# Four attention layers on one core: the range test and its branch moved to the end, loads reordered, masks and normalisations moved from POOL to DVE

## Chip, cores and metric

One core of a Trainium2 chip (trn2). The metric is the device time of one execution in microseconds (us), median of several runs; the profile is of one execution. TensorE is called PE, its weight loads PEld, VectorE DVE, ScalarE ACT, GpSimd POOL, and SyncE, which issues most DMAs, SP; a q behind an engine's name (SPq) marks its sequencer, here mostly for the issue of a DMA. "Slot" is a step of the kernel's own software pipeline in an A layer: a group of four heads takes six slots, and a segment of 512 tokens has eight groups G.

## The reference, cut to what matters

```python
x = A_x                                              # 2048 tokens x 640, bf16
x = x + _A_ref(_layernorm(x), wq, wk, wv, wo, beta)  # 4 segments of 512, 32 heads of 20, causal,
x = x + _B_ref(_layernorm(x), mem0, Wq, Wk, Wv, Wo)  #   plus a linear memory gated by sigmoid(beta)
x = x + _A_ref(_layernorm(x), ...)                   # B: 64 steps of 32 tokens, 32 heads of 128,
x = x + _B_ref(_layernorm(x), ...)                   #   8 memory tokens carried from step to step
```

The B layers are a chain of 64 steps each; the A layers have a short chain of four segments. A segment needs the LayerNorm of its 512 tokens, transposed, before its first projection.

## The kernel before

It first computes from wq and wk a bound on the scores. If the bound holds, exponentials need no row maximum, and each A layer branches to a short arm:

```python
# in prep_A: pad wq and wk to 32 columns per head, sums of squares on POOL and DVE, ... (cut)
flag = tp_.tile([1, 1], mybir.dt.int32, name="a_flag")
nc.vector.tensor_copy(flag[:], b2[:])
W.bounded = nc.values_load(flag[0:1, 0:1])
...
# at the end of layer_A
with tc.If(W.bounded > 0) as arm:
    run(False, None)
with arm.Else():
    ...
```

In an A layer the next segment's LayerNorm is threaded through the groups of this one. `tt` counts its four tiles of 128 tokens. Statistics are made on DVE, the power -0.5 on POOL, the normalisation on POOL, the transposes on PE:

```python
def ln_stats(nc, xt):
    ...                                    # two bn_stats, bn_aggr, add eps, all on DVE
    nc.gpsimd.tensor_tensor(out=rstd[:], in0=rstd[:], in1=C.mhalf[:, 0:1], op=ALU.pow)
    return mv, rstd
...
for tt in range(4):
    if (G, slot) == (tt + 1, 1):
        ln[tt] = ln_load(n + 1, tt)
    if (G, slot) == (tt + 2, 2):
        mv, rstd = ln_stats(nc, ln[tt])
        ln[tt] = ln_apply(nc.gpsimd, ln[tt], mv, rstd)
    if (G, slot) == (tt + 3, 4):
        ln_tr(nc, ln.pop(tt), n + 1, tt)
```

Inside the layers the kernel pins each compute engine's order of instructions to the order of these lines; DMA issues are left to the compiler's scheduler. The causal mask is applied to the exponentials by POOL, in four selects for each pair of heads (one, one and two for the three parts of the scores):

```python
nc.scalar.activation(out=PT[:], in_=Sx[:, :, 0:N], func=ACT.Exp, scale=SC)
for c0 in ((0,), (0,), (0, 256))[part]:
    v = PT[:, :, c0:c0 + 128]
    nc.gpsimd.affine_select(out=v, in_=v, ...)
```

A B layer begins with its 5 MB output weight and only then asks for its first tokens:

```python
nc.sync.dma_start(WB.wo[:], B_Wo.rearrange("h e d -> e h d"))   # in the caller
layer_B(...)                # its start: ln_dma(0); ln_norm(0); ln_tr(0)
```

## Time and profile before

Before the prediction the kernel took 3148.21 us (median of 3 runs, 3141.85 to 3148.53). I cut the span at four kinds of event, each of them twice: the first projection a_PP of an A layer, the end of its last output matmul a_YP, the first b_Qa of a B layer and the end of its last b_OPSd.

| stretch | us before |
|---|---|
| start, to the first a_PP | 61.7 |
| first A layer | 303.2 |
| A to B, first time | 58.8 |
| first B layer | 1158.7 |
| B to A | 33.1 |
| second A layer | 306.6 |
| A to B, second time | 60.9 |
| second B layer | 1159.1 |
| end | 5.6 |

The names in the profiles: a_xt is a tile of x, a_xn its normalised form, a_tps the transposes of that on PE; a_PP are the projections, a_S the scores, a_PT the exponentials, a_VP and a_vaug the values, a_pv their product with a_PT, a_YP the output matmul and a_xo its sum with x, a_UP the update of the memory. In B, b_xt and b_lntps are what a_xt and a_tps are in A.

The start, from the timeline of the kernel before. The columns are start, duration, engine, line, operation, output and inputs, shape and count; in brackets the idle time before it and what ended it.

```profile
8.11 15.77 DVE L135 COPY a_pad_100<-a_raw_98 128x640 bf16<-128x640 bf16 x3 [1.96 <-DMA a_raw_98<-in_A_wq_dram]
...
32.58 0.14 DVE L151 CAST a_flag<-a_b_144 1x1 int32<-1x1 f32 x1
...
43.16 2.51 POOL L228 TENSOR_SCALAR a_xn<-a_xt,a_mv,a_rstd 128x640 bf16<-128x640 bf16 x1 [0.25 <-POOL a_rstd L223]
...
61.66 2.10 PE L84 MATMUL a_PP<-a_xnT_193,a_wt 128*128 128x512 bf16 x9 [0.24 <-PE a_VP L241]
```

Padding and the bound take 33 us before anything of the attention begins, and LayerNorm, half of it on POOL, follows.

The two A layers before, in the view of windows (stretch, its length, busy time of each engine, granted PE clock, share of DMA, GB/s):

```profile
core 0: us, PE busy (x) PEld busy (x) DVE busy (x) ACT busy (x) POOL busy (x), PEclk, DMA share, GB/s
61.70:364.90 303.20, 265.34 (x2789) 139.30 (x2818) 170.85 (x416) 200.19 (x272) 179.56 (x358) 0.91 0.41 133
1615.50:1922.20 306.70, 265.40 (x2789) 138.89 (x2818) 171.57 (x416) 200.40 (x272) 180.54 (x359) 0.92 0.32 98
```

What PE and the weight loads waited for in the first A layer before, besides "issue" (view of waits: engine and what it waited for, us in total, times, longest):

```profile
PEld L84 <- POOL a_PT L84: 28.7, 76, 1.5
PE a_pv L84 <- POOL a_PT L84: 13.8, 35, 1.2
```

These are POOL's selects.

The change from A to B before, timeline:

```profile
373.46 0.39 SPq L1041 DMA_DIRECT2D b_wo<-in_B_Wo_dram  x1
374.03 9.31 SPq L617 DMA_DIRECT2D b_xt<-xres_bf  x1
...
391.49 0.89 DVE L84 BATCH_NORM_STATS2 b_ln_st<-b_xt 128x6 f32<-128x320 bf16 x2 [16.90 <-DMA b_xt<-xres_bf]
...
394.10 0.69 PE L84 MATMUL b_lntps<-c_identb,b_xt 128*128 128x128 bf16 x5 [29.25 <-DMA b_XOd<-xres]
```

The tile b_xt is asked for just after Wo and lands 17 us later; PE stands for 29 us.

### The profile page before, as it was taken

To read this page: it belongs to the slowest core of one execution; us is meant where nothing else is said; L and a number is where in the kernel's file an instruction comes from. 1 tells how busy PE (TensorE), PEld (TensorE's weight loads), DVE (VectorE), ACT (ScalarE), POOL (GpSimd) and SP (SyncE) were. 2 spreads that over 40 slices of the span, in tenths; PEclk is the share of its full clock that TensorE was granted. 3 is DMA by queue.
4 is the path that set the end of the run, shared out by engine and by line. 5 is a ranking of instruction groups with operands and counts; after the bars stand their busy time and mean duration, and the time that the engine had idled before them with its cause. 6 is when DMAs were issued, how large, how long until landed. Compare 5 with 4: busy or idle time off the path is not lost. (4 is left out here: it accounts for less than half of the span.)

```text
span 3147.7 us, 118684 instructions
## 1 busy us (share of the span) xinstructions
PE 2734.2 (87%) x52376; PEld 1461.4 (46%) x52438; DVE 1626.5 (52%) x4137; ACT 1328.7 (42%) x2798; POOL 756.3 (24%) x1975
## 2 busy tenths in 40 slices
PE   3889479999999999999868884899999999999997
PEld 1444235545555454455434442445455455455554
DVE  5665335555555555555446652455555555555554
ACT  2766324443433443433337662343433433434432
POOL 4666311111111111111136652111111111111111
PEclk9998789999999999999979995999999999999998
DMA  4633400000000000000023333000000000000000
GB/s 165 213 97 98 131 14 17 19 18 18 18 17 18 19 17 18 17 18 16 13 85 118 114 97 108 12 16 16 16 15 16 16 15 16 15 16 17 13 14 10
DMA packets 110982, 134.33 MB, mean 43 GB/s; under 512 B 30704, under 2 KB 96240, under 8 KB 108528
## 3 DMA queue, kind: packets, MB, share of 16 engines
q1 hardware_dynamic: 110304, 126.55, 13.9%
q8 instruction: 414, 6.78, 0.9%
q14 instruction: 120, 0.98, 0.1%
q10 hardware_dynamic: 144, 0.01, 0.0%
HBM read 91.84 MB, written 26.25 MB: 38 GB/s over the span
## 5 line engine op out<-in xcount | busy, mean ns | idle before, releaser
L84 PEld LDWEIGHTS <-b_hT 128*32 128x32 bf16 x15520 | 355.5, 96 | 375.7 <-DVE b_hT L84 46.5
L84 POOL TENSOR_TENSOR b_P<-b_Pu,b_rs 128x256 bf16<-128x256 bf16 (+1 forms) x256 | 111.6, 457 | 1180.0 <-DVE b_rs L84 1172.7
L84 ACT ACTIVATE a_PT<-a_S 128x768 bf16<-128x768 f32 (+1 forms) x384 | 328.8, 888 | 103.8 <-PE a_S L84 91.4
L84 PE MATMUL b_OPS<-b_wo,b_OTsb 128*32 128x320 bf16 x8192 | 317.5, 310 | 44.7 <-DVE b_OTsb L84 44.7
L84 PE MATMUL b_V<-b_wv,b_hT 128*32 128x512 bf16 x5120 | 346.8, 382 | 0.0
L84 PEld LDWEIGHTS <-b_OTsb 128*32 128x32 bf16 x8192 | 212.8, 99 | 118.5 <-DVE b_OTsb L84 58.3
L84 ACT ACTIVATE b_Pu<-b_SP 128x320 bf16<-128x320 f32 x256 | 112.0, 437 | 357.0 <-DVE b_SP L84 357.0
L84 POOL TENSOR_SCALAR_AFFINE_SELECT a_PT<-a_PT 128x256 bf16<-128x256 bf16 x512 | 207.2, 425 | 175.6 <-ACT a_PT L84 173.3
L84 ACT COPY b_QT<-b_TPQ 128x128 bf16<-128x128 bf16 x508 | 178.2, 379 | 119.7 <-PE b_TPQ L84 115.9
L84 DVE COPY b_KT<-b_TPK 128x128 bf16<-128x128 bf16 x382 | 101.8, 267 | 217.9 <-PE b_TPK L84 217.9
L84 PE MATMUL b_Qa<-b_wq,b_hT 128*32 128x512 bf16 x2560 | 163.5, 384 | 34.7 <-DVE b_hT L84 34.7
L84 DVE CAST b_hT<-b_MT 128x24 bf16<-128x24 f32 x126 | 23.1, 183 | 329.6 <-PE b_MT L84 329.6
L84 ACT CAST b_msb<-b_OPS 128x320 bf16<-128x320 f32 x128 | 54.5, 426 | 296.1 <-PE b_OPS L84 296.1
L84 POOL COPY b_OTdef<-b_OTsb 128x256 bf16<-128x256 bf16 x128 | 51.0, 399 | 509.0 <-DVE b_OTsb L84 509.0
L84 DVE CAST b_Ksb<-b_Ka 128x512 bf16<-128x512 f32 x128 | 88.6, 692 | 149.0 <-PE b_Ka L84 148.8
L84 PE MATMUL b_Ka<-b_wk,b_hT 128*32 128x512 bf16 x2560 | 161.8, 382 | 0.0
L84 PE MATMUL b_Kb<-b_wk,b_hT 128*32 128x512 bf16 x2560 | 161.6, 381 | 0.0
L84 DVE TENSOR_REDUCE b_negmax<-b_SP 128x8 f32<-128x320 f32 x256 | 124.8, 487 | 71.1 <-PE b_SP L84 71.1
L84 DVE TENSOR_REDUCE b_ssum<-b_Pu 128x8 f32<-128x320 bf16 x256 | 123.2, 481 | 72.4 <-ACT b_Pu L84 72.4
L84 PE MATMUL b_Qb<-b_wq,b_hT 128*32 128x512 bf16 x2560 | 160.3, 379 | 0.0
L84 ACT ACTIVATE b_Qsb<-b_Qb 128x512 bf16<-128x512 f32 x128 | 76.4, 597 | 197.2 <-PE b_Qb L84 197.2
L84 DVE CAST b_Ksb<-b_Kb 128x512 bf16<-128x512 f32 x128 | 88.6, 692 | 125.8 <-PE b_Kb L84 125.8
(224 smaller groups left out, 5105.0 us busy)
## 6 DMA issues: line engine op xcount, KB each, us to landing
b_wo<-in_B_Wo_dram SPq DMA_DIRECT2D x2, 5120.0 KB
b_Vt<-b_Vtb SPq DMA_DIRECT2D x512, 16.0 KB
b_XO<-xres SPq DMA_DIRECT2D x256, 30.0 KB
a_wvo<-in_A_wo_dram SPq DMA_DIRECT2D x8, 800.0 KB
b_wq<-in_B_Wq_dram SPq DMA_DIRECT2D x5, 1024.0 KB
b_wk<-in_B_Wk_dram SPq DMA_DIRECT2D x5, 1024.0 KB
b_wv<-in_B_Wv_dram SPq DMA_DIRECT2D x5, 1024.0 KB
xres<-a_xo SPq DMA_DIRECT2D x16, 320.0 KB
```

The source lines that it names most:

```text
L84: r = f(*a, **k)
```

## The change

The intent: no test and no branch ahead of the work. The sums of exponentials and their inverses are totalled as the A layers run, and tested at the very end; if one is out of range, all four layers are done again with row maxima. Around this the loads are reordered (x first; in B the tokens ahead of Wo), the pads are used from SBUF in the first layer, and DVE takes work from POOL: two of the four selects become one minimum with a 0-or-huge mask, and the normalisations. The normalisation is also placed one group later, and its load five slots later. The core of the diff, cut:

```diff
+def watch(nc, C, sums, inverses):
+    n = sums.shape[1]
+    nc.gpsimd.tensor_tensor(out=C.tot[:, 0, 0:n], in0=C.tot[:, 0, 0:n], in1=sums, op=ALU.add)
+    nc.gpsimd.tensor_tensor(out=C.tot[:, 1, 0:n], in0=C.tot[:, 1, 0:n], in1=inverses, op=ALU.add)
 ... (cut: pads filled after the first LayerNorms, out_of_range() with a matmul over C.tot and a value load)
-                for c0 in ((0,), (0,), (0, 256))[part]:
+                if part == 2 and not general:
+                    v = PT[:].rearrange("p j (b q) -> p j b q", q=128)[:, :, 0:3:2, :]
+                    nc.vector.tensor_tensor(out=v, in0=v, in1=tri[:]..., op=ALU.min)
+                for c0 in ((0,), (0,), (0, 256) if general else ())[part]:
 ... (cut)
-                        if (G, slot) == (tt + 1, 1):
+                        if (G, slot) == (tt + 2, 0):
                             ln[tt] = ln_load(n + 1, tt)
-                        if (G, slot) == (tt + 2, 2):
+                        if (G, slot) == (tt + 3, 2):
                             mv, rstd = ln_stats(nc, ln[tt])
-                            ln[tt] = ln_apply(nc.gpsimd, ln[tt], mv, rstd)
+                            ln[tt] = ln_apply(nc.vector, ln[tt], mv, rstd)
                         if (G, slot) == (tt + 3, 4):
                             ln_tr(nc, ln.pop(tt), n + 1, tt)
 ... (cut: layer_B)
-        ln_dma(0); ln_norm(0); ln_tr(0)
+        ln_dma(0)
+        m0 = wk.tile([8, D], BF16, name="b_m0", tag="OTsb")
+        nc.sync.dma_start(m0[:], mem0)
+        for q in range(4):
+            nc_raw.sync.dma_start(W.wo[:, 8 * q:8 * q + 8, :], wo_src[:, 8 * q:8 * q + 8, :])
+        ln_norm(0); ln_tr(0)
 ... (cut: full_kernel)
+        run(False)
+        with tc.If(out_of_range(nc, tc, C) > 0):
+            run(True)
```

More of the change, by code (lines that the diff above doesn't have):

```diff
@@ L52, in build_consts @@
     nc.vector.memset(C.mhalf[:], -0.5)
+    C.tot = cp.tile([128, 2, 16], F32, name="c_tot")
+    nc.vector.memset(C.tot[:], 0.0)
     tctx.close()
@@ L102, in __getattr__, with out_of_range @@
         return getattr(self._nc, attr)
+def watch(nc, C, sums, inverses):
+    n = sums.shape[1]
+    nc.gpsimd.tensor_tensor(out=C.tot[:, 0, 0:n], in0=C.tot[:, 0, 0:n], in1=sums, op=ALU.add)
+    nc.gpsimd.tensor_tensor(out=C.tot[:, 1, 0:n], in0=C.tot[:, 1, 0:n], in1=inverses, op=ALU.add)
+def out_of_range(nc, tc, C):
+    with ExitStack() as tctx:
+        tp_ = tctx.enter_context(tc.tile_pool(name="c_range", bufs=1))
+        pp = tctx.enter_context(tc.tile_pool(name="c_range_ps", bufs=1, space=PSUM))
+        ok = tp_.tile([128, 32], F32, name="c_ok")
+        nc.vector.tensor_scalar(out=ok[:], in0=C.tot[:].rearrange("p k n -> p (k n)"), scalar1=1e30, scalar2=None, op0=ALU.is_le)
+        ones = tp_.tile([128, 1], F32, name="c_one")
+        nc.vector.memset(ones[:], 1.0)
+        ps = pp.tile([1, 32], F32, name="c_okps")
+        nc.tensor.matmul(ps[:], lhsT=ones[:], rhs=ok[:], start=True, stop=True)
+        n = tp_.tile([1, 1], F32, name="c_n")
+        nc.vector.tensor_reduce(out=n[:], in_=ps[:], axis=AX.X, op=ALU.add)
+        nc.vector.tensor_scalar(out=n[:], in0=n[:], scalar1=-1.0, scalar2=128.0 * 32, op0=ALU.mult, op1=ALU.add)
+        flag = tp_.tile([1, 1], mybir.dt.int32, name="c_flag")
+        nc.vector.tensor_copy(flag[:], n[:])
+        return nc.values_load(flag[0:1, 0:1])
@@ L105, with prep_A, fill @@
 class AWeights:
     pass
-def prep_A(nc, tc, C, A_wq, A_wk, A_beta):
-    SC = 1.0 / math.sqrt(20.0)
-    W = AWeights()
-    W.gates = tc.dram_tile([128, 64], F32, name="a_gates")
-    W.wpad = [tc.dram_tile([2, 128, NCH * 128], BF16, name=f"a_wpad{G}") for G in range(8)]
-    with ExitStack() as tctx:
-        tp_ = tctx.enter_context(tc.tile_pool(name="a_prep", bufs=1))
-        pp = tctx.enter_context(tc.tile_pool(name="a_prep_ps", bufs=1, space=PSUM))
-        bb = tp_.tile([128, 32], BF16, name="a_beta_bf")
-        with nc.allow_non_contiguous_dma(reason="beta bcast"):
-            nc.scalar.dma_start(bb[:], A_beta.partition_broadcast(128))
-        hs = tp_.tile([128, 2, 32], F32, name="a_hs")
-        for k, src in enumerate((A_wq, A_wk)):
-            raw = tp_.tile([128, NCH, D], BF16, name=f"a_raw{k}")
-            nc.sync.dma_start(raw[:], src.rearrange("(c p) n -> p c n", p=128))
-            pad = tp_.tile([128, 8, NCH, 4, 32], BF16, name=f"a_pad{k}")
-            nc.gpsimd.memset(pad[:], 0.0)
+def prep_A(nc, tc, W, space, A_wq, A_wk, A_beta):
+    raw = space[:, 0:2 * NCH * D].rearrange("p (k c n) -> p k c n", k=2, c=NCH)
+    n0 = 2 * NCH * D
+    pad = space[:, n0:n0 + 2 * NCH * 1024].rearrange("p (k g c h s) -> p k g c h s", k=2, g=8, c=NCH, h=4)
+    for k in range(2):
+        nc.gpsimd.memset(pad[:, k, :, :, :, 20:32].rearrange("p g c h s -> p (g c h) s"), 0.0)
+    for k, src in enumerate((A_wq, A_wk)):
+        nc.scalar.dma_start(raw[:, k], src.rearrange("(c p) n -> p c n", p=128))
+    W.pad = [[pad[:, k, G].rearrange("p c h s -> p c (h s)") for k in range(2)] for G in range(8)]
+    def fill():
+        for k in range(2):
@@ L129, in prep_A @@
             for c in range(NCH):
-                dst = pad[:, :, c, :, 0:20]
-                s_ = raw[:, c, :].rearrange("p (g h d) -> p g h d", g=8, d=20)
-                if c % 2:
+                dst = pad[:, k, :, c, :, 0:20]
+                s_ = raw[:, k, c, :].rearrange("p (g h d) -> p g h d", g=8, d=20)
+                if c % 3 == 1:
                     nc.scalar.copy(dst, s_)
@@ L135, in prep_A @@
                     nc.vector.tensor_copy(dst, s_)
-            for G in range(8):
-                nc.sync.dma_start(W.wpad[G][k], pad[:, G].rearrange("p c h d -> p (c h d)"))
-            sq = tp_.tile([128, NCH, D], F32, name=f"a_sq{k}")
-            nc.gpsimd.tensor_tensor(out=sq[:], in0=raw[:], in1=raw[:], op=ALU.mult)
-            nc.vector.tensor_reduce(out=hs[:, k, :], in_=sq[:].rearrange("p c (h d) -> p h c d", d=20), axis=AX.XY, op=ALU.add)
-        ones = tp_.tile([128, 1], F32, name="a_ones")
@@ L142, in prep_A @@
-        nc.vector.memset(ones[:], 1.0)
-        hp = pp.tile([1, 2, 32], F32, name="a_hp")
-        nc.tensor.matmul(hp[:], lhsT=ones[:], rhs=hs[:].rearrange("p k h -> p (k h)"), start=True, stop=True)
-        mx = tp_.tile([1, 2], F32, name="a_mx")
-        nc.vector.tensor_reduce(out=mx[:], in_=hp[:], axis=AX.X, op=ALU.max)
-        b2 = tp_.tile([1, 1], F32, name="a_b2")
-        nc.vector.tensor_tensor(out=b2[:], in0=mx[:, 0:1], in1=mx[:, 1:2], op=ALU.mult)
-        nc.vector.tensor_scalar(out=b2[:], in0=b2[:], scalar1=(40.0 / (1.02 * 640.0 * SC)) ** 2, scalar2=None, op0=ALU.is_le)
@@ L150, in prep_A @@
-        flag = tp_.tile([1, 1], mybir.dt.int32, name="a_flag")
-        nc.vector.tensor_copy(flag[:], b2[:])
-        W.bounded = nc.values_load(flag[0:1, 0:1])
-        e = tp_.tile([128, 32], F32, name="a_beta_e")
-        nc.scalar.activation(out=e[:], in_=bb[:], func=ACT.Exp, scale=-1.0)
-        nc.vector.tensor_scalar(out=e[:], in0=e[:], scalar1=1.0, scalar2=None, op0=ALU.add)
-        gg = tp_.tile([128, 2, 32], F32, name="a_gg0")
-        nc.vector.reciprocal(out=gg[:, 1, :], in_=e[:])
+        for G in range(8):
+            for k in range(2):
+                nc.sync.dma_start(W.wpad[G][k], pad[:, k, G].rearrange("p c h s -> p (c h s)"))
@@ new lines, in gates @@
+    def gates(pool):
+        bb = pool.tile([128, 32], BF16, name="a_beta_bf")
+        with nc.allow_non_contiguous_dma(reason="beta bcast"):
+            nc.scalar.dma_start(bb[:], A_beta.partition_broadcast(128))
+        gg = pool.tile([128, 2, 32], F32, name="a_gg")
+        nc.scalar.activation(out=gg[:, 0, :], in_=bb[:], func=ACT.Exp, scale=-1.0)
+        nc.vector.tensor_scalar(out=gg[:, 0, :], in0=gg[:, 0, :], scalar1=1.0, scalar2=None, op0=ALU.add)
+        nc.vector.reciprocal(out=gg[:, 1, :], in_=gg[:, 0, :])
@@ L158, in prep_A, with layer_A @@
         nc.vector.tensor_scalar(out=gg[:, 0, :], in0=gg[:, 1, :], scalar1=-1.0, scalar2=1.0, op0=ALU.mult, op1=ALU.add)
-        nc.sync.dma_start(W.gates[:], gg[:].rearrange("p k h -> p (k h)"))
-    return W
-def layer_A(nc_raw, tc, C, W, A_wv, A_wo, x_src, x_dst, xb_dst, src_is_bf16, prefetch=()):
+        return gg
+    W.gates = gates
+    return fill
+def layer_A(nc_raw, tc, C, W, A_wv, A_wo, x_src, x_dst, xb_dst, src_is_bf16, general, prep=None, prefetch=()):
     SC = 1.0 / math.sqrt(20.0)
@@ L182, in layer_A @@
         phik = [st.tile([128, 4, 4, 32], BF16, name=f"a_phik{i}") for i in range(2)]
-        for i in range(2):
-            nc_raw.gpsimd.memset(vaug[i][:, :, :, 20:22], 1.0)
-            nc_raw.gpsimd.memset(phik[i][:], 0.0)
         xnTs = [st.tile([128, NCH, 512], BF16, name=f"a_xnT{i}") for i in range(2)]
@@ L192, in load_vo, with wload @@
             nc_raw.sync.dma_start(wvo[:], src.rearrange("(c p) n -> p c n", p=128))
-        load_vo(A_wv)
-        bd = st.tile([128, 4, 21], BF16, name="a_bd")
-        nc_raw.vector.memset(bd[:], 0.0)
-        for j in range(4):
-            nc_raw.vector.memset(bd[32 * j:32 * j + 32, j, :], 1.0)
-        eps = st.tile([128, 2, 4, 4], F32, name="a_eps")
-        nc_raw.vector.memset(eps[:, 0], 0.0)
-        nc_raw.vector.memset(eps[:, 1], 1e-6)
-        gg = st.tile([128, 2, 32], F32, name="a_gg")
-        nc_raw.sync.dma_start(gg[:].rearrange("p k h -> p (k h)"), W.gates[:])
         class Seg:
             pass
+        def wload(u):
+            if prep and u < NG:
+                wts[u] = W.pad[u]
+                return
+            wt = wk.tile([128, 2, NCH, 128], BF16, name="a_wt")
+            for k in range(2):
+                nc_raw.sync.dma_start(wt[:, k].rearrange("p c m -> p (c m)"), W.wpad[u % NG][k])
+            wts[u] = [wt[:, 0], wt[:, 1]]
         def ln_load(n, tt):
@@ L243, in vproj @@
             nc.vector.tensor_copy(vaug[n % 2][:, tt, 16 * half:16 * half + 16, 0:20], VP[:].rearrange("p (h d) -> p h d", d=20))
-        for tt in range(4):
-            xt = ln_load(0, tt)
-            mv, rstd = ln_stats(nc_raw, xt)
-            ln_tr(nc_raw, ln_apply((nc_raw.vector, nc_raw.gpsimd)[tt % 2], xt, mv, rstd), 0, tt)
+        xts = [ln_load(0, tt) for tt in range(2)]
+        fill_pads = prep() if prep else None
+        load_vo(A_wv)
+        wts = {}
+        if not prep:
+            wload(0); wload(1)
+        for i in range(2):
+            nc_raw.gpsimd.memset(vaug[i][:, :, :, 20:22], 1.0)
+            nc_raw.gpsimd.memset(phik[i][:], 0.0)
+        tri = st.tile([128, 128], BF16, name="a_tri")
+        nc_raw.vector.memset(tri[:], 3.0e38)
+        nc_raw.gpsimd.affine_select(out=tri[:], in_=tri[:], pattern=[[1, 128]], compare_op=ALU.is_ge,
+                                    fill=0.0, base=0, channel_multiplier=-1)
+        for tt in range(4):
+            if tt + 2 < 4:
+                xts.append(ln_load(0, tt + 2))
+            mv, rstd = ln_stats(nc_raw, xts[tt])
+            ln_tr(nc_raw, ln_apply(nc_raw.vector, xts[tt], mv, rstd), 0, tt)
+        if fill_pads:
+            fill_pads()
         for tt in range(4):
@@ L251, in layer_A, with run @@
                 vproj(nc_raw, 0, tt, half)
-        def run(general, gctx):
+        bd = st.tile([128, 4, 21], BF16, name="a_bd")
+        nc_raw.vector.memset(bd[:], 0.0)
+        for j in range(4):
+            nc_raw.vector.memset(bd[32 * j:32 * j + 32, j, :], 1.0)
+        eps = st.tile([128, 2, 4, 4], F32, name="a_eps")
+        nc_raw.vector.memset(eps[:, 0], 0.0)
+        nc_raw.vector.memset(eps[:, 1], 1e-6)
+        gg = W.gates(st)
+        def run(gctx):
             nc = _OrdNC(tc, nc_raw, engines=ORDER_ENGINES)
@@ L266, in run @@
                 nc.vector.memset(ones[:], 1.0)
-            wts, us, xin = {}, {}, {}
-            def wload(u):
-                wt = wk.tile([128, 2, NCH, 128], BF16, name="a_wt")
-                for k in range(2):
-                    nc_raw.sync.dma_start(wt[:, k].rearrange("p c m -> p (c m)"), W.wpad[u % NG][k])
-                wts[u] = wt
+            us, xin = {}, {}
             def proj(u, k):
@@ L283, in proj @@
                 for c in range(NCH):
-                    nc.tensor.matmul(PP[:], lhsT=wts[u][:, k, c, :], rhs=xnTs[n % 2][:, c, :], start=(c == 0), stop=(c == NCH - 1))
+                    nc.tensor.matmul(PP[:], lhsT=wts[u][k][:, c, :], rhs=xnTs[n % 2][:, c, :], start=(c == 0), stop=(c == NCH - 1))
                 nc.vector.tensor_copy(U.qk[:, k, :], PP[:])
@@ L354, in score @@
                 nc.scalar.activation(out=PT[:], in_=Sx[:, :, 0:N], func=ACT.Exp, scale=SC)
-                for c0 in ((0,), (0,), (0, 256))[part]:
+                if part == 2 and not general:
+                    v = PT[:].rearrange("p j (b q) -> p j b q", q=128)[:, :, 0:3:2, :]
+                    nc.vector.tensor_tensor(out=v, in0=v, in1=tri[:].unsqueeze(1).unsqueeze(1).to_broadcast([128, 2, 2, 128]), op=ALU.min)
+                for c0 in ((0,), (0,), (0, 256) if general else ())[part]:
                     v = PT[:, :, c0:c0 + 128]
@@ L393, in norm @@
                 nc.vector.tensor_tensor(out=r[:, 0:K], in0=pv[:, 0:K, :, :, 20], in1=eps[:, 0:K], op=ALU.add)
-                nc.vector.reciprocal(out=r[:, 0:K], in_=r[:, 0:K])
-                nc.vector.tensor_tensor(out=r[:, 0:K], in0=r[:, 0:K], in1=gg[:, 0:K, 4 * G:4 * G + 4].unsqueeze(2).to_broadcast([128, K, 4, 4]), op=ALU.mult)
+                i = wk.tile([128, 2, 4, 4], F32, name="a_i")
+                nc.vector.reciprocal(out=i[:, 0:K], in_=r[:, 0:K])
+                if not general:
+                    watch(nc, C, r[:, 0].rearrange("p t j -> p (t j)"), i[:, 0].rearrange("p t j -> p (t j)"))
+                q = wk.tile([128, 2, 4, 4], F32, name="a_q")
+                nc.vector.tensor_tensor(out=q[:, 0:K], in0=i[:, 0:K], in1=gg[:, 0:K, 4 * G:4 * G + 4].unsqueeze(2).to_broadcast([128, K, 4, 4]), op=ALU.mult)
                 Ov = Onat[:, :, 80 * G:80 * G + 80].rearrange("p t (j d) -> p t j d", d=20)
                 if n == 0:
-                    nc.vector.tensor_tensor(out=Ov, in0=pv[:, 0, :, :, 0:20], in1=r[:, 0].unsqueeze(3).to_broadcast([128, 4, 4, 20]), op=ALU.mult)
+                    nc.vector.tensor_tensor(out=Ov, in0=pv[:, 0, :, :, 0:20], in1=q[:, 0].unsqueeze(3).to_broadcast([128, 4, 4, 20]), op=ALU.mult)
                 else:
@@ L401, in norm @@
                     nc.vector.tensor_tensor(out=ts[:].rearrange("p k t d -> p (k t) d"), in0=pv[:].rearrange("p k t j s -> p (k t j) s")[:, :, 0:20],
-                                            in1=r[:].rearrange("p k t j -> p (k t j)").unsqueeze(2).to_broadcast([128, 32, 20]), op=ALU.mult)
+                                            in1=q[:].rearrange("p k t j -> p (k t j)").unsqueeze(2).to_broadcast([128, 32, 20]), op=ALU.mult)
                     tv = ts[:].rearrange("p k (t j) d -> p k t j d", j=4)
@@ L489, in extras @@
                     load_vo(A_wo)
-            wload(0); wload(1)
+            if prep:
+                wload(0); wload(1)
             proj(0, 0); proj(0, 1); phi_q(0); phi_k(0)
@@ L524, in run @@
                     extras(u, slot)
-        with tc.If(W.bounded > 0) as arm:
-            run(False, None)
-        with arm.Else():
-            with ExitStack() as gctx:
-                run(True, gctx)
+        with ExitStack() as gctx:
+            run(gctx)
 class BWeights:
@@ L555, in b_slot_of_head, with layer_B @@
     return j, j + 4 * (2 * b + r // 2), r % 2
-def layer_B(nc, tc, C, W, x_src, xb_src, x_dst, mem0, nsteps=64, out_bf16=False):
+def layer_B(nc, tc, C, W, wo_src, x_src, xb_src, x_dst, mem0, nsteps=64, out_bf16=False):
     SCB = 1.0 / math.sqrt(128.0)
@@ L571, in layer_B @@
         wk = st
+        wop = ctx.enter_context(tc.tile_pool(name="b_wo", bufs=1))
+        W.wo = wop.tile([128, 32, D], BF16, name="b_wo")
         pp = ctx.enter_context(tc.tile_pool(name="b_ps", bufs=8, space=PSUM))
@@ L780, in layer_B @@
         assert sorted(HORDER) == list(range(32))
-        ln_dma(0); ln_norm(0); ln_tr(0)
+        ln_dma(0)
[4 more added lines that the diff above has]
+        ln_norm(0); ln_tr(0)
         alloc_h(0)
-        with nc.allow_non_contiguous_dma(reason="mem0 transpose load (tiny)"):
-            for c in range(NCH):
-                nc.sync.dma_start(hT[0][:, c, 24:32], mem0[:, 128 * c:128 * c + 128].rearrange("t p -> p t"))
+        mt = ps_tile([128, NCH, 8], BF16, "b_m0T")
+        for c in range(NCH):
+            nc.tensor.transpose(mt[:, c, :], m0[0:8, 128 * c:128 * c + 128], C.identb[0:8, 0:8])
+        nc.vector.tensor_copy(hT[0][:, :, 24:32], mt[:])
         alloc_qk(0)
@@ L1025, in full_kernel @@
         mem0 = B_mem0.rearrange("b t d -> (b t) d")
+        wo_src = B_Wo.rearrange("h e d -> e h d")
         X = tc.dram_tile([S_TOK, D], F32, name="xres")
@@ L1028, in full_kernel, with prep, run @@
         WB, loads = load_B_weights(nc, tc, ctx, B_Wq, B_Wk, B_Wv)
-        WA = prep_A(nc, tc, C, A_wq, A_wk, A_beta)
-        nl = len(layers)
-        assert layers[0] == "A" and layers[-1] == "B"
-        for li, L in enumerate(layers):
-            lastl = (li == nl - 1)
-            if L == "A":
-                layer_A(nc, tc, C, WA, A_wv, A_wo, xin if li == 0 else X, X, Xb, li == 0, prefetch=loads)
-                loads = []
-            else:
-                with ExitStack() as bctx:
-                    wop = bctx.enter_context(tc.tile_pool(name="b_wo", bufs=1))
-                    WB.wo = wop.tile([128, 32, D], BF16, name="b_wo")
-                    nc.sync.dma_start(WB.wo[:], B_Wo.rearrange("h e d -> e h d"))
-                    layer_B(nc, tc, C, WB, X, Xb, xout if lastl else X, mem0, out_bf16=lastl)
+        WA = AWeights()
+        WA.wpad = [tc.dram_tile([2, 128, NCH * 128], BF16, name=f"a_wpad{G}") for G in range(8)]
+        def prep():
+            return prep_A(nc, tc, WA, WB.wv[:].rearrange("p c n -> p (c n)"), A_wq, A_wk, A_beta)
+        def run(general):
+            nl = len(layers)
+            assert layers[0] == "A" and layers[-1] == "B"
+            for li, L in enumerate(layers):
+                lastl = (li == nl - 1)
+                if L == "A":
+                    first = li == 0 and not general
+                    layer_A(nc, tc, C, WA, A_wv, A_wo, xin if li == 0 else X, X, Xb, li == 0, general,
+                            prep=prep if first else None, prefetch=loads if first else ())
+                else:
+                    layer_B(nc, tc, C, WB, wo_src, X, Xb, xout if lastl else X, mem0, out_bf16=lastl)
+        run(False)
+        with tc.If(out_of_range(nc, tc, C) > 0):
+            run(True)
 @with_exitstack
```

## The prediction

> **What bounds the kernel now.** The program is four layers, A B A B (table by stretch, timeline). PE is busy 87% of the span and 92% or more inside B, whose 18.1 us steps the change does not touch. So it can pay only at the start, at the three layer changes, and inside A (about 290 us each; PE 81 to 90%, POOL 55 to 68%, DVE 55 to 63%).
>
> **Removed or moved, costed from the timeline:**
>
> 1. *Start.* PE's first projection begins at 61.7 us: 33 us of bound test, pad copies and branch value, then loads, then LayerNorm, half of it on POOL (2.5 us each; DVE 0.45). Three DVE pad copies took 15.8 us beside POOL work. [...] Afterwards x is loaded first, without a test. But the order of instructions shows two 1 MB b_wq loads ahead of the third and fourth x tiles, and the wq/wk loads behind the beta exponential. First projection at 27 to 35 us: **-30 us**.
>
> 2. *A to B, twice.* B's first LayerNorm waits 17 us for a 160 KB tile queued behind the 5 MB Wo load; PE is idle from 364.9 to 394.1 and from 1922.3 to 1949.5 us. Afterwards the tile comes first, and the branch region's barrier and jump are gone. The order still puts the last bf16 cast on POOL, which waits for a store (3.5 us), before B's first power, so about 7 us of gap stay: **-46 us** for both, with a little clock. TensorE is granted 0.5 in these gaps, and 20 matmuls take 2.32 us instead of 1.26 after them[...]. The remaining gap still throttles.
>
> 3. *B to A.* 1582.4 to 1615.5 us. Two x tiles are requested earlier, LayerNorm is all on DVE; the other two still queue behind Wv, which waits for the last stores: **-8 us**.
>
> 4. *Inside A.* Per group POOL loses four of eight selects (0.42 us each) and the 2.5 us normalisations, and gets two small totals (about 0.3 us each, estimated from the 0.36 us memory update). DVE gets two minima (0.45 to 0.8 us each, estimated from the 0.43 us phi minimum) and normalisations of 0.45 to 0.6: roughly 75% busy. PE and weight loads waited for POOL selects 30 to 40 us per A layer (view of waits), but ACT and the full PE stand behind: **-15 us** over both layers, uncertain from -45 to +15.
>
> 5. *End.* The test waits for the last stores, then DVE, PE, DVE, a value load and a branch over the second copy. From the old test (31.6 to 33.8 us) and the 2.3 us jump after an A layer: **+5 us**.
>
> Sum: -94 us. **Predicted 3052 us, 8 in 10 between 3015 and 3085.** Chances: faster by over 2% 0.90, within 2% 0.09, slower 0.01.
>
> **What would show it.** First a_PP matmul near 31 us; b_lntps 6 to 9 us after the last a_YP; first a_PP of the second A about 25 us after the last b_OPSd; POOL about 45% in A, DVE about 75%; B steps still 18.1 us; 4 to 7 us after the last output store.
>
> **What would make it wrong.** DVE becoming A's bottleneck through in-order waits for ACT[...]; late b_wv loads waiting for the pads and holding other loads on their queue; a larger A gain if the clock's dips to 0.83 there come from POOL stalls; a costlier final branch.

The marked cuts take out reasons that no trace or run of this case shows. They take no term out of the sum: -30 - 46 - 8 - 15 + 5 = -94 us.

## The result, and the profile after

The kernel after took 3102.76 us (median of 4 runs, 3099.93 to 3103.3), the kernel before in the same comparison 3145.03 us (3140.91 to 3148.53). The ratio is 0.9864, with a 95% interval of 0.9847 to 0.9881: within 2%, and a gain of 42 us in place of the 94 predicted. Here and below a ratio is the mean time of one kernel's runs over the mean of the other's in the same rounds, so not quite the ratio of the medians quoted. Executions over 1.5% slower than the fastest of the same kernel are left out of the means.

| stretch | before | after | difference | predicted |
|---|---|---|---|---|
| start | 61.7 | 31.7 | -30.0 | -30 |
| first A | 303.2 | 313.4 | +10.2 | -15 for both A |
| A to B | 58.8 | 38.1 | -20.7 | -46 for both |
| first B | 1158.7 | 1158.0 | -0.7 | 0 |
| B to A | 33.1 | 28.4 | -4.7 | -8 |
| second A | 306.6 | 317.4 | +10.8 | (above) |
| A to B | 60.9 | 40.4 | -20.5 | (above) |
| second B | 1159.1 | 1160.0 | +0.9 | 0 |
| end | 5.6 | 12.8 | +7.2 | +5 |

The differences add up to -47.5 us, which is the difference of the two profiled spans, 3147.7 and 3100.2. Four of the five terms are within 5 us of the prediction. The A layers went the other way.

The A layers after, view of windows; the columns are as above:

```profile
core 0: us, PE busy (x) PEld busy (x) DVE busy (x) ACT busy (x) POOL busy (x), PEclk, DMA share, GB/s
31.70:345.10 313.40, 269.72 (x2821) 139.96 (x2819) 197.76 (x492) 198.94 (x272) 116.84 (x282) 0.88 0.35 117
1569.60:1887.00 317.40, 269.49 (x2821) 140.41 (x2819) 199.78 (x491) 198.99 (x272) 119.14 (x283) 0.88 0.31 95
```

POOL's work fell from 180 to 117 us and DVE's rose from 171 to 198 (63% of the stretch), as intended. Yet the stretch is longer, and the granted clock is lower. The waits of the first A layer after:

```profile
PEld L86 <- DVE a_xn L86: 27.6, 12, 2.9
PE a_tps L86 <- DVE a_vaug L86: 14.2, 6, 3.0
PE a_tps L86 <- DVE a_xn L86: 8.8, 4, 2.7
PE a_tps L86 <- DVE a_xo L86: 5.6, 2, 2.8
PEld L86 <- POOL a_PT L86: 1.4, 8, 0.2
```

The waits for POOL's selects are nearly gone (28.7 to 1.4 us). In their place stand twelve new ones: the transposes a_tps of the next segment's x. The three lines of a_tps are one wait under three names, put down to whichever DVE instruction came last: 14.2 + 8.8 + 5.6 = 28.6 us in twelve waits, which is 4 tiles for each of the 3 segments that follow. One of them in the timeline after:

```profile
137.11 0.38 PE L86 MATMUL a_KN<-c_identb,a_qk 128*128 128x128 bf16 x4
137.37 0.88 DVE L86 BATCH_NORM_STATS2 a_st<-a_xt 128x6 f32<-128x320 bf16 x2
...
138.53 0.15 DVE L86 TENSOR_SCALAR a_rstd<-a_mv 128x1 f32<-128x1 f32 x1
138.76 0.55 POOL L86 TENSOR_TENSOR a_rstd<-a_rstd,c_mhalf 128x1 f32<-128x1 f32 x1 [1.91 <-DVE a_rstd L86]
...
139.35 0.51 DVE L86 TENSOR_SCALAR a_xn<-a_xt,a_mv,a_rstd 128x640 bf16<-128x640 bf16 x1 [0.66 <-POOL a_rstd L86]
139.78 0.48 DVE L86 TENSOR_TENSOR a_xo<-a_YP,a_xr 128x320 f32<-128x320 f32 x1
...
139.91 0.10 PEld L86 LDWEIGHTS <-a_xn 128*128 128x128 bf16 x1 [2.59 <-DVE a_xn L86]
...
140.31 0.69 PE L86 MATMUL a_tps<-c_identb,a_xn 128*128 128x128 bf16 x5 [2.81 <-DVE a_xo L86]
...
142.60 2.31 PE L86 MATMUL a_PP<-a_xnT,a_wt 128*128 128x512 bf16 x5
```

From 137.37 to 139.86 us a chain runs from DVE to POOL and back to DVE, and PE, which has reached its transposes, does nothing for 2.8 us. The last 0.4 us of them go to the instruction behind the chain on DVE: the weight load of a_xn begins at 139.91, the transposes only at 140.31, right after a_xo. Then PE is slow: five a_PP matmuls take 2.31 us, where other groups of five take 1.25 in the same trace. The windows around it:

```profile
136.00:140.00 4.00, 1.50 (x29) 0.97 (x28) 3.23 (x10) 1.94 (x3) 1.77 (x3) 0.97 0.75 207
140.00:144.00 4.00, 3.69 (x23) 1.81 (x24) 1.82 (x5) 2.43 (x3) 1.91 (x5) 0.50 0.85 285
```

The granted clock is 0.50 from 140 to 144 us. Finer windows have 1.00 up to 139.7, 0.50 from 139.8 on, when PE had paused for 2.3 us of the 2.8, and 0.99 again from 146.6. In windows of 1 us the clock falls to 0.50 at eleven of the first A layer's twelve waits, within 2 us of the start of the transposes; at the first of them (62.2 us) it stays at 1.00. Nor is a low clock found at such pauses alone. The kernel before, too, ran its A layers at 0.91 and 0.92, and in the 283 us from the first a_PP on no pause of its PE is longer than 1.2 us; yet one of its windows reads

```profile
252.00:262.00 10.00, 9.72 (x91) 4.98 (x91) 5.31 (x15) 5.54 (x9) 6.96 (x12) 0.62 0.12 34
```

What else the clock follows is not shown.

The change from A to B after, and the end after, timeline:

```profile
345.20 0.32 SPq L648 DMA_DIRECT2D b_xt<-xres_bf  x1
...
349.81 0.89 DVE L86 BATCH_NORM_STATS2 b_ln_st<-b_xt 128x6 f32<-128x320 bf16 x2 [1.86 <-DMA b_XOd<-xres]
...
351.66 6.46 SPq L818 DMA_DIRECT2D b_wo<-in_B_Wo_dram  x4
...
352.45 0.69 PE L86 MATMUL b_lntps<-c_identb,b_xt 128*128 128x128 bf16 x5 [7.32 <-DVE b_xt L86]
...
3088.52 2.64 SPq L1045 DMA_DIRECT2D out_dram<-b_xnbd  x8
3092.49 0.18 DVE L120 TENSOR_SCALAR c_ok<-c_tot 128x32 f32<-128x32 f32 x1 [4.00 <-DMA out_dram<-b_xnbd]
...
3093.58 0.14 DVE L129 CAST c_flag<-c_n 1x1 int32<-1x1 f32 x1
```

b_xt goes first and PE's pause is 7.3 us in place of 29.3. At the end the test waits 4.0 us for the last stores, and 6.5 us follow its flag (3093.7 to 3100.2): value loads of about 0.5 us, the branch, and the program's end. The branch instruction is short on four engines (0.05 to 0.07 us) and long on PE's sequencer. In the view of its line (count; shortest, median and longest in ns; first and last start):

```profile
L1086 PEldq COMPARE_BRANCH  x1: 3402/3402/3402, 3094.6 to 3094.6; - x1
```

### The profile page after: what moved, and what is told of

Read it like the earlier page. It is cut to its first block, busy times and chain, and to the rows that moved or that the text cites. A ratio compares the mean times of both kernels' runs of the same rounds, so it can differ in the third digit from the quotient of the medians.

```text
span 3100.2 us, 118652 instructions
## 1 busy us (share of the span) xinstructions
PE 2744.0 (89%) x52448; PEld 1465.0 (47%) x52448; DVE 1662.4 (54%) x4299; ACT 1326.2 (43%) x2799; POOL 606.1 (20%) x1819
## 5 line engine op out<-in xcount | busy, mean ns | idle before, releaser
L86 PE MATMUL a_PP<-a_xnT,a_wt 128*128 128x512 bf16 x560 | 156.3, 415 | 2.1 <-DVE a_t1k L86 0.9
L86 POOL TENSOR_SCALAR_AFFINE_SELECT a_PT<-a_PT 128x256 bf16<-128x256 bf16 x256 | 109.8, 433 | 213.5 <-ACT a_PT L86 200.4
```

Of the source, the lines that this page charges most:

```text
L86: r = f(*a, **k)
```

## The experiments

Theory 1: the normalisation now stands two slots ahead of the transposes that need it, and these waits, with the clock they cost, are the loss in A. Theory 2: DVE is overloaded by the minima. Theory 3: the totals hold up POOL. Theory 4: the clock alone. Twelve runs, each of five rounds against the kernel before; all gave correct results. "A" below is both A layers together, between the same events as above: 609.9 us before, 630.8 after.

**e1_late_transposes.** After, with later transposes:

```diff
-                        if (G, slot) == (tt + 3, 4):
+                        if (G, slot) == ((tt + 4, 1) if tt < 3 else (6, 5)):
```

> The kernel after, but PE's transposes of the next segment's normalised x come later: three slots later for the first three tiles of a segment, one slot later for the fourth; everything else unchanged. Theory 1 (the normalisation, moved to two slots ahead of its transposes, makes PE wait about 3 us for DVE 12 times in each A layer, and the TensorE clock dips behind each wait): the weight load's wait for a_xn falls from 27.6 us in a layer to under 8, both A layers shorten by 15 to 30 us each, time 3045 to 3070 us against 3102. Theory 2 (DVE is overloaded by the mask minima): the waits for DVE come back elsewhere and the time stays at 3092 to 3105. Theory 3 (the totals of sums on POOL) and theory 4 (the clock alone): as theory 2.

Measured: 3081.02 us (3079.34 to 3093.31), ratio to before 0.9795. A is 611.1 us. The direction is theory 1's, but the gain is half of what I expected. The waits for a_xn are gone (no line of them is left among PEld's first seven), but others came, in the first A layer:

```profile
PE a_UP L86 <- DVE a_vaug L86: 10.8, 7, 2.5
PE a_VP L86 <- DVE a_t1k L86: 5.9, 3, 2.2
PE a_UP L86 <- DVE a_xo L86: 4.6, 2, 2.3
```

DVE still runs statistics, the wait for POOL and the normalisation in one block of 2.5 us, and whatever stands behind it in DVE's order is late. The timeline of this run has the block and one of the waits:

```profile
134.84 0.88 DVE L86 BATCH_NORM_STATS2 a_st<-a_xt 128x6 f32<-128x320 bf16 x2
...
136.82 0.51 DVE L86 TENSOR_SCALAR a_xn<-a_xt,a_mv,a_rstd 128x640 bf16<-128x640 bf16 x1 [0.66 <-POOL a_rstd L86]
...
137.25 0.48 DVE L86 TENSOR_TENSOR a_xo<-a_YP,a_xr 128x320 f32<-128x320 f32 x1
...
137.78 0.45 PE L86 MATMUL a_UP<-a_vaug,a_phik 128*128 128x84 bf16 x4 [2.28 <-DVE a_xo L86]
```

What a_UP waits for is a_xo, which reads a_YP; in the program a_YP and a_UP take their PSUM buffers from one pool. So theory 1 has to be widened: the block delays PE, through the transposes or through what follows it on DVE.

**e2_early_statistics.** After, with the block split and moved ahead:

```diff
-                        if (G, slot) == (tt + 2, 0):
+                        if (G, slot) == (tt + 1, 1):
                             ln[tt] = ln_load(n + 1, tt)
-                        if (G, slot) == (tt + 3, 2):
-                            mv, rstd = ln_stats(nc, ln[tt])
-                            ln[tt] = ln_apply(nc.vector, ln[tt], mv, rstd)
+                        if (G, slot) == (tt + 2, 2):
+                            ln[tt] = (ln[tt],) + ln_stats(nc, ln[tt])
+                        if (G, slot) == (tt + 3, 0):
+                            ln[tt] = ln_apply(nc.vector, *ln[tt])
```

> The kernel after, but the load and the statistics of a tile come one group earlier, where they stood in the kernel before, and the normalisation on DVE two slots earlier; transposes unchanged. Theory 1: as for the run with later transposes, all 12 waits of a layer gone (the fourth tile's too), time 3040 to 3065 us. Theories 2, 3 and 4: 3092 to 3105 us.

Measured: 3043.64 us (3040.11 to 3050.89), ratio 0.9669 (0.9656 to 0.9683): faster than before by 3.3%, and 59 us below after. Theories 2, 3 and 4 said 3092 or more, with the same minima and totals, and fall. The A layers of this run, view of windows:

```profile
32.00:317.50 285.50, 251.81 (x2791) 135.79 (x2819) 196.04 (x492) 198.28 (x272) 116.24 (x282) 0.94 0.38 128
1545.20:1834.20 289.00, 253.18 (x2796) 136.81 (x2825) 198.88 (x493) 197.97 (x272) 116.88 (x283) 0.94 0.33 104
```

A is 574.5 us (the second window lies 1.3 us early; cut at its events it gives 0.2 us more). Its 56.3 us against after split into PE's idle time, 91.6 to 69.5 us (-22.1), and PE's busy time, 539.2 to 505.0 us (-34.2), for the same matmuls at a clock of 0.94 in place of 0.88. The trace of e2 lacks 31 of the 320 a_PP records of each A layer, which that of after has; by the holes that they leave, an estimate, about 3 us of the 34 are idle time by this gap in the record alone. More than half of what the late place cost was still paid in slower matmuls. Not all twelve are gone: a_tps still waits 4.8 + 3.0 us in the first A layer (28.6 after), so the expectation "all 12 gone" is not quite met; the time is near the lower end of what was expected.

**e3_before_with_shift.** The same shift put into the kernel before, which has no minima and no totals:

```diff
-                        if (G, slot) == (tt + 1, 1):
+                        if (G, slot) == (tt + 2, 0):
                             ln[tt] = ln_load(n + 1, tt)
-                        if (G, slot) == (tt + 2, 2):
+                        if (G, slot) == (tt + 3, 2):
                             mv, rstd = ln_stats(nc, ln[tt])
-                            ln[tt] = ln_apply(nc.gpsimd, ln[tt], mv, rstd)
+                            ln[tt] = ln_apply(nc.vector, ln[tt], mv, rstd)
```

> The kernel before with one part of the change alone: the load, statistics and normalisation of a tile moved to the change's places, and the normalisation on DVE instead of POOL. Theory 1: PE gets the same 12 waits for a_xn in a layer, so although POOL loses 2.5 us of work for each tile the time rises by 20 to 60 us, to 3165 to 3205. Theory 2 and 3: no waits of PE for a_xn, POOL relieved, 3120 to 3148 us.

Measured: 3195.22 us (3186.04 to 3198.4), ratio 1.015 (1.0137 to 1.0163). A is 647.2 us, 37 more than before, although POOL has less to do. The first A layer's waits:

```profile
PEld L84 <- DVE a_xn L84: 20.2, 12, 2.0
```

This part of the change alone makes the kernel slower by 47 us, as theory 1 said.

**e4_selects_back.** After, with the third part's minimum turned back into two POOL selects:

```diff
-                if part == 2 and not general:
+                if False:
 ...
-                for c0 in ((0,), (0,), (0, 256) if general else ())[part]:
+                for c0 in ((0,), (0,), (0, 256))[part]:
```

> The kernel after with the third part's causal mask again as two selects on POOL instead of a minimum on DVE. Theory 1: the 12 waits for a_xn stay, POOL's selects hold PE again as before (a_PT waits of PE and weight loads above 20 us a layer), time 3110 to 3150 us. Theory 2: DVE is relieved of 256 minima, the time falls to 3060 to 3090 us.

Measured: 3125.62 us (3120.54 to 3131.22), ratio 0.9929. A is 657.1 us. In the first A layer the weight loads wait 19.1 us for a_xn, 12 times, and 23.2 us for a_PT from POOL, as theory 1 said. Relieving DVE made it slower: theory 2 falls again. (The minima taken off DVE are 64 in an A layer, 128 in all, not the 256 of the expectation.)

**e5_early_selects_back.** The edits of e2 and e4 together.

> The run with early statistics, with the third part's mask again as two POOL selects. It prices the minima where no PE wait for a_xn hides them. Theory 1 (the selects of POOL were a real wait of PE, and the change's minima remove it): PE's and the weight loads' waits for a_PT from POOL come back to 25 to 40 us in an A layer, each A layer 8 to 18 us longer than with early statistics alone, time 3060 to 3080 us against 3044. Rival (DVE loaded too much by the minima): the same or faster, 3030 to 3046 us.

Measured: 3066.92 us (3066.1 to 3068.73), ratio 0.9748. A is 598.1 us, and in the first A layer PEld waits 23.3 and a_pv 13.5 us for a_PT from POOL again. With e2, e4 and after this is a square, whose effects very nearly add:

| A, us | two selects on POOL | minimum on DVE | the minimum's gain |
|---|---|---|---|
| normalisation late (as after) | 657.1 (e4) | 630.8 (after) | 26.3 |
| early (e2) | 598.1 (e5) | 574.5 (e2) | 23.6 |
| the late place costs | 59.0 | 56.3 | |

Each entry is from one profile; that of e4 is of a run 5.5 us above its median. The medians of the whole times make nearly the same square: the minimum gains 22.9 and 23.3 us, the late place costs 58.7 and 59.1.

**e6_early_no_totals.** e2 without the totals:

```diff
-                if not general:
+                if False:
                     watch(nc, C, ...)
```

> The run with early statistics, without the totals of sums and inverses (the test at the end reads zeros, so it always says in range; right for these inputs only). Theory 1: the totals are two POOL operations of 0.22 us for each of 64 groups, beside an engine that is a third busy: at most 6 us faster, 3037 to 3046 us. Theory 3 (the totals on POOL hold up the selects and the power): over 12 us faster, below 3032 us.

Measured: 3055.35 us (3054.66 to 3057.64), ratio 0.971: 12 us *slower* than e2, which nobody expected. A is 585.2 us, of it PE busy 512.2 (e2: 505.0) and idle 73.0 (69.5); the clock is 0.92 and 0.93. Theory 3 falls: the totals cost nothing that can be seen. Why less work on POOL goes with a lower clock stays open (e2 also ran on another chip, but the kernel before took 3148.13 and 3147.07 us beside the two). I take from it that a difference of about 10 us between two arrangements of A is not evidence for either.

**e7_early_no_test.** e6, and also without the test, the branch and the second copy of the layers:

```diff
-        with tc.If(out_of_range(nc, tc, C) > 0):
-            run(True)
```

> The run with early statistics, without the totals and without the test, the branch and the second copy of the layers at the end (no fallback at all; right for these inputs only). If the end costs what the trace says (14.5 us from the last b_OPSd matmul to the end of the span against 5.6 in the kernel before), the time is 7 to 11 us below the run without totals alone, the last stretch 4 to 7 us, and no other stretch moves by over 1 us.

Measured: 3049.39 us (3047.42 to 3050.82), ratio 0.9691, 6 us below e6, just outside the 7 to 11. The last stretch fell from 14.9 to 5.8 us (-9.1), so test and branch cost about 9 us at the end. That other stretches do not move was wrong: A -1.6, the second A to B 35.5 to 39.7.

**e8_before_load_order.** Before, with B's first tile and memory ahead of Wo in four parts, as in the change:

```diff
-                    nc.sync.dma_start(WB.wo[:], B_Wo.rearrange("h e d -> e h d"))
 ...
-        ln_dma(0); ln_norm(0); ln_tr(0)
+        ln_dma(0)
+        ...  # m0 load, four Wo loads, PE transposes of m0, as in the change
+        ln_norm(0); ln_tr(0)
```

> The kernel before with one part alone: at the start of B the first LayerNorm tile and the memory tokens are loaded ahead of Wo, Wo in four parts, the memory transposed on PE. If the order of the loads makes the gain at the two changes from A to B (58.8 and 60.9 us before, 38.1 and 40.4 after), each gap falls to 38 to 46 us and the time to 3106 to 3126 us. Rival (the branch around the layer and its barrier made the gap): gaps stay above 52 us, time 3136 to 3148 us.

Measured: 3131.59 us (3126.88 to 3139.13), ratio 0.9957. The gaps are 52.6 and 49.8 us (58.8 and 60.9 before), between the two theories. The views of the timeline and of the branch's line show why:

```profile
L526 SPq COMPARE_BRANCH  x1: 43/43/43, 371.8 to 371.8; - x1
374.53 1.13 SPq L787 DMA_DIRECT2D b_wo<-in_B_Wo_dram  x2
375.78 1.39 SPq L617 DMA_DIRECT2D b_xt<-xres_bf  x1
```

Two of the four Wo loads were issued ahead of b_xt; the compiler's scheduler, and not the order of the lines, had placed them. And SP comes to the branch at the end of A only at 371.8 us, after it has issued A's last stores, so that b_xt is asked for 9.9 us after the last a_YP (365.9). In after, without a branch there, it is asked for 0.1 us after it (345.2 and 345.1), ahead of A's last stores. So the branch region, too, kept the tile back: of the 14.5 us by which this first gap is longer than that of after, 9.8 are the later request.

**e9_after_wo_first.** After, with Wo in one piece written ahead of the first tile:

```diff
+        nc.sync.dma_start(W.wo[:], wo_src)
         ln_dma(0)
         ...
-        for q in range(4):
-            nc_raw.sync.dma_start(W.wo[:, 8 * q:8 * q + 8, :], wo_src[:, 8 * q:8 * q + 8, :])
```

> The kernel after with one part undone: at the start of B the 5 MB of Wo are loaded again in one piece, ahead of the first LayerNorm tile. The run that put the order alone into the kernel before took only 6.2 and 11.1 us off the two gaps. Theory (the order makes about half of the gain, the vanished branch region the other half): each gap from A to B grows from 38 to 40 us to 46 to 54 us, time 3118 to 3132 us against 3102. Rival (with the branch gone the order is worth nothing): gaps 38 to 42 us, 3100 to 3107 us.

Measured: 3107.45 us (3105.34 to 3108.67), ratio 0.9874; gaps 38.0 and 40.2 us. Inconclusive: in its timeline b_xt is still issued at 348.6 us and Wo at 355.0, so the edit did not undo what it was to undo. It shows only that the four parts are worth nothing against one.

**e10_early_start_gates.** e2, with two waits removed:

```diff
-    identf = ...                          # f32 identity in a temporary, cast to bf16
+    nc.gpsimd.affine_select(out=C.identb[:], in_=C.identb[:], ...)      # in bf16, in place
-        xts = [ln_load(0, tt) for tt in range(2)]                       # two more in the loop
+        xts = [ln_load(0, tt, tt >= 2) for tt in range(4)]              # tiles 2, 3 in a_xr buffers
-        gg = W.gates(st)                                                # ahead of run()
+            gg = W.gates(nc, st, bb)                                    # after the first proj, phi_k
```

> The run with early statistics, and two waits seen in the trace of after removed: at the start all four x tiles are requested at once (two in idle buffers) and the identity is made in bf16 directly, so that the wq and wk loads need not wait for the f32 temporary; the gates are computed after the first projections instead of inside the first LayerNorms. If these waits set the two stretches, the first a_PP falls from 32.0 to 22 to 27 us and the stretch from B to A from 28.6 to 22 to 26 us, time 3026 to 3038 us against 3044; if others stand behind them, both move by under 2 us.

Measured: 3034.09 us (3028.73 to 3036.61), ratio 0.964. The start is 24.0 us (e2: 32.0) and B to A 21.8 us (28.6), as expected, the second by 0.2 us better. This answers what stood in the B to A stretch after:

```profile
1550.68 0.36 ACTq L164 DMA_DIRECT2D a_beta_bf<-in_A_beta_dram  x1
...
1555.74 0.18 DVE L167 TENSOR_SCALAR a_gg<-a_gg 128x32 f32<-128x32 f32 x1 [5.14 <-ACT a_gg L166]
...
1556.43 0.48 DVE L223 BATCH_NORM_STATS2 a_st<-a_xt 128x6 f32<-128x320 f32 x1
```

These are lines of the kernel after: a gate that is not yet needed waits 5.1 us on DVE for a load of 32 numbers, and the third tile's statistics stand behind it.

**e11_early_flag.** e10, with the flag computed between the last A and the last B layer:

```diff
+                if lastl and not general:
+                    out_of_range(nc, tc, C)          # now writes C.flag
 ...
-        with tc.If(out_of_range(nc, tc, C) > 0):
+        with tc.If(nc.values_load(C.flag[0:1, 0:1]) > 0):
```

> The previous run, and the flag of the test is computed between the last A and the last B layer into a tile that lives on; only its load and the branch stay at the end. The last stretch falls from 14 to 15 us to 7 to 11 us, the change from A to B before it grows by under 2 us, time 3 to 7 us below the previous run.

Measured: 3029.52 us (3027.34 to 3036.58), ratio 0.9635 (0.9616 to 0.9655). The last stretch is 11.3 us (e10: 15.4), the A to B ahead of it 41.1 (40.1). The stretch moved as expected, if 0.3 us short of it; the two times can't be told apart, as their ranges overlap. This is the fastest version measured, 3.65% faster than before by the ratio.

**e12_after_wo_forced.** e9 with an ordering edge that the scheduler must respect:

```diff
+        first = nc_raw.sync.dma_start(W.wo[:], wo_src)
+        ln_dma(0, first)     # tc.add_manual_dep(load.ins, first.ins.name, ..., reason="order")
```

> The kernel after with Wo ahead of the first LayerNorm tile at the start of B, this time with an ordering edge from one load to the other (in the earlier run the compiler's scheduler put the tile ahead again, so that the edit did nothing). If the order of the loads is what counts, the tile lands 14 to 17 us after Wo is issued (at about 352 us in the trace of after), b_lntps begins near 368 instead of 352 us, each gap from A to B grows from 38 to 40 us to 50 to 57 us, time 3126 to 3140 us against 3102. If the vanished branch region made the whole gain, the gaps stay within 3 us and the time below 3109 us.

Measured: 3144.7 us (3144.49 to 3146.58), ratio 0.9994 (0.998 to 1.0008). The gaps are 60.1 and 58.0 us. The timeline of the first:

```profile
353.96 0.40 SPq L816 DMA_DIRECT2D b_wo<-in_B_Wo_dram  x1
354.40 20.75 SPq L648 DMA_DIRECT2D b_xt<-xres_bf  x2
371.47 0.89 DVE L86 BATCH_NORM_STATS2 b_ln_st<-b_xt 128x6 f32<-128x320 bf16 x2 [20.98 <-DMA b_xt<-xres_bf]
```

The tile lands 17 us after it is asked for, 160 KB behind the 5 MB of Wo. Undoing the order gives back 22.0 + 17.6 = 39.6 of the 41.2 us that the two changes of layer had gained. The size was above what I expected. So the order is needed for nearly all of that gain: without it the gain is gone, although no branch region is left. (PE's pause ahead of b_lntps grows from 7.3 to 26.4 us. Of these 19.1 us, 6.7 pass before b_xt is issued, since Wo itself is issued only 6.3 us after the last a_YP; the rest is the longer way behind Wo.) That the branch region counted for nothing does not follow, as e8 shows: the order could pay in full only where the tile can also be asked for early.

## Why the prediction was wrong, point by point

- *Start, -30 predicted, -30.0 measured.* Right, and so was its place near 31 us. e10 shows that 8 us more were to be had from the wq/wk loads and x tiles that the prediction had named as late. For wq and wk the wait was another than it named: in after they are issued at 6.93 us, right after the cast of the identity ends (6.90), while the beta exponential had ended at 4.68. That DVE's pad copies were long because of POOL was read from the trace of before (0.3 to 10 us each): the first two took 9.98 and 5.63 us while POOL was busy from 8.09 to 23.46 us, the four that began after that 0.31 to 0.32; no run tested it.
- *A to B, -46 predicted, -41.2 measured.* Right, and it had named both parts: e12 shows that the gain needs the order of the loads, e8 that with the branch region still there the tile is asked for 9.8 us later. b_lntps was predicted 6 to 9 us after the last a_YP and came after 7.3. The clock did fall in the gap that remains: 0.50 from 349 to 364 us.
- *B to A, -8 predicted, -4.7 measured.* Mis-sized by 3 us: the gates stood in DVE's order ahead of the third tile's statistics, 5.1 us. e10, which moved them, also asked for all four x tiles at once; the 6.8 us that it took off this stretch are not divided between the two.
- *End, +5 predicted, +7.2 measured; B, 0 predicted, +0.2 measured.* Right. e7 put test and branch at 9.1 us; the branch on PE's sequencer takes 3.4 us in after.
- *Inside A, -15 predicted, +20.9 measured.* This is the step that failed. The prediction counted what POOL loses and DVE gains, as amounts of work, and concluded "ACT and the full PE stand behind". It did not count the distance between a result and its reader. The normalisation was moved a whole group later, its transposes were not moved, and only two slots were left for a chain of three turns, DVE, POOL and DVE. With the square above, and e5 against before (598.1 - 609.9), the sum is: all else that the change does inside A (normalisation on DVE in place of POOL, the totals, pads from SBUF in the first layer, no branch around the layer), -11.8 us; the minimum, -23.6; the late place, +56.3. That is +20.9, the measured figure (630.8 - 609.9). The sum has to close, since the terms share their runs; what the runs show is the size of each. The first term is near the 10 us that e6 makes me distrust, and no run takes it apart; the other two are well above. So the relief of POOL was larger than predicted (24 us from the minimum alone, not 15 in all; perhaps 35 with the first term), and more than all of it was given back by a wait that nothing in the prediction priced.
- *Which of its warnings came true.* The prediction feared DVE as a bottleneck through in-order waits. DVE's load was not the matter (63% busy, 75% expected; e4 and e5 relieve it and are slower), its order was: the 2.5 us block, e1. POOL was 37% busy, 45% expected. And the clock added to the pauses: of the 56 us, 31 to 34 are slower matmuls. That each of them follows from a pause is not shown, since the clock also fell where no pause was long (0.62 in the window of before above).
- *Open.* Why e6 and e7, without the totals, have longer A layers than e2, and what lowers the clock where PE has no long pause.

## What to carry to other kernels

When a change moves a producer, put its new place beside its consumer's in the pinned orders of the engines and add up the chain between them, also through other engines; the busy shares (here 63% of DVE, 37% of POOL) do not show it. Here short pauses of PE, repeated (twelve in the first A layer, 28.6 us together), went with a lower clock (0.88 in after, 0.94 in e2) that cost more than the idle time itself (31 to 34 us against 22 to 25): price such a pause by the stretch, not by the idle line. And look in the trace at where a reordered DMA was really issued before believing an experiment on its order: twice here the scheduler had undone the edit, in part (e8) or wholly (e9).
